# The opening of a fused Fourier-mixing and SiLU kernel: other buffers, another order and more filler products

## The chip, the core and the metric

The kernel runs on one core of one Trainium2 chip. The metric is the device time of one execution in microseconds (us). A core has TensorE (PE in the profile, its weight loads apart as PEld), VectorE (DVE), ScalarE (ACT), GpSimd (POOL), SyncE (SP, which here only issues transfers), and 16 DMA engines. An engine takes its instructions in the order in which the program gives them. ACT and POOL issue transfers too, and an issue that has to wait holds up what stands behind it on that engine.

## What is computed

```python
X = np.fft.rfft(x, axis=1)                      # x: 8 batches x 3008 x 256, float32
y = np.fft.irfft(X * (filt_r + 1j * filt_i)[None], n=3008, axis=1)
h = y.reshape(24064, 256) @ w_in                # w_in: 256 x 2048
out = (h / (1 + np.exp(-h))) @ w_out            # w_out: 2048 x 256
```

So each batch is filtered along its 3008 positions, and all 24064 rows then go through a two-layer network with SiLU between the layers.

## The kernel before, in words

**The body.** Each batch is cut into 6 pairs of token blocks (`PAIRS` for each half), and each pair is taken through 8 steps (`NJP`), one for each block of 256 hidden columns: 384 steps in all. A step is `hidden` (L639, seven products of 128x128 weights by 256 columns, a Strassen-like scheme with seven weight combinations for each 2x2 block) and `project` of the step before (L698, seven more). The combinations come from `combine_weights` (four additions or subtractions of 128x256; with `part` 0 or 1 it makes the first or the last two). While the steps of one batch run, the transform of the next is threaded between them: `put` and `plan` give each piece a step and an eighth of a step (a "round"), and `until` issues what is due.

**The transform of a batch** has four kinds of product: stage 1 (`pa`), `forward` (`pb`, L433), inverse (`pc`, L491) and `stage3` (`pd`, L538). Between `forward` and inverse, `multiply` (L448) takes the filter to the PSUM results, and between inverse and `stage3` the results go through DRAM (`d2`) to be regrouped.

**The opening** is what the change is about: batch 0 has no steps to hide behind. Its groups g = 0 to 5 go through these pieces, in an order written out by hand (L957 to L1013):

- `multiply(g, k)` for k = 0, 1 on DVE: a real and an imaginary filter product of 128x512 each, into a tile of the pool `z` (4 buffers) and one of the pool `p` (2 buffers; for k = 1 one of the pool `abc`).
- `inverse_first(g)` on PE: 16 products for each of 4 terms and 2 halves (groups 2 to 5), which read those tiles.
- `rows_first(g)`: for i = 0, 1 ACT copies a 128x512 result out of PSUM (L498) into a tile of the pool `q` (i = 0) or `o` (i = 1), 2 buffers each, and issues its store to `d2` (L501, 256 KB), on the ACT queue; for group 4 on the POOL queue.
- `load_t4(g, first, last)`: loads back, for g = 0 to 3, rows `first` to `last` of `d2` (L526). Rows 0 to 31 come from groups 0 to 3, rows 32 to 47 from groups 4 and 5. All issues are on the SP queue, but for one of the two halves of the last rows, which is on the ACT queue. The tiles for g = 2 and 3 stand where `neg[0]` and `neg[1]`, two tables of `inverse_first`, stood.
- `stage3(g)` for g = 0 to 3, and copies of its results to `y` (L549 on ACT, for g = 2 and 3 one on DVE L244 and one on ACT L246). With all eight copied, step 0 can begin.

**Weights.** The 16 blocks j of the weights come as raw float64 words. `load_weights(j)` (L816, L819) loads two halves of 256 KB each on SP; `split_weights` (DVE L835, L838; ACT L837, L839, and for some L844, L845), `round_weights` (DVE L851 to L857) and `place_weights` (L866) turn them into float32 in `w_t`. Blocks 0 and 1 are loaded into a tile of the pool `y`, blocks 2 and 3 into its other buffer. Their work is put between the pieces of the opening: `split(4, 5)` stands behind `inverse_first(5)` and ahead of `rows_first(3)`, and `combine_weights` of 0 and 1 are on POOL.

**x of batch 1.** `second["load_x"](u)` loads 384 KB into half `u` of `x_all` (L274, on SP). A `memset` of one element by POOL (L976) stands ahead of it. Stage 1 of batch 0 had its own last x in `x_all`, read for the last time by the L297 products that end at 29.42 us.

**Filler.** `idle(n)` (L918) makes n products of 96x128 by 128 whose result nobody reads. `idle(36)` stands at the start, `idle(20)` ahead of `stage3(0)`.

**PSUM.** In the opening `bank` hands out the eight banks in turn.

Of the kernel before, what the change touches and what calls it, by code (L numbers as in the profile page):

```python
# [46 lines left out]
FP32 = mybir.dt.float32  # L47
# [6 lines left out]
B, S, C = 8, 3008, 256  # L54
DFF = 2048
N1, N2 = 47, 64
NS, NG = 24, 6
# [110 lines left out]
def kernel(  # L168
# [31 lines left out]
    zpool = pool("z", 4)  # L200
# [22 lines left out]
    x_all = xpool.tile([128, 2, 2, 2 * C], FP32)  # L223
# [26 lines left out]
    def bank(b, name, spare=None):  # L250


        if b > 0 and spare is not None:
            return accps.tile([128, 2, C], FP32, name=name, tag=f"a{spare}")
        if b > 0 or early[0] is None:
            return fps.tile([128, 2, C], FP32, name=name, tag="f")
        early[0] += 1
        k = early[0] % 8
        if k < 2:
            return fps.tile([128, 2, C], FP32, name=name, tag="f")  # L260
        if k > 5:
            return xps.tile([128, 2, C], FP32, name=name, tag="x" if k == 6 else "yz")
        return accps.tile([128, 2, C], FP32, name=name, tag=f"a{k - 2}")

    def spectral(b):
# [4 lines left out]
        xs, us, t2s, banks, prods, halves, t4s = {}, {}, {}, {}, {}, {}, {}  # L270
# [168 lines left out]
            prods[g] = []  # L439

        def multiply(g, k):
            z = zpool.tile([128, 2, C], FP32, name=f"z_{b}_{g}_{k}", tag="z")
            if b == 0 and k == 1:
                pt = abcpool.tile([128, 3, C], FP32, name=f"p_{b}_{g}_{k}", tag="abc")[:, 0:2]
            else:
                pt = ppool.tile([128, 2, C], FP32, name=f"p_{b}_{g}_{k}", tag="p")
            for m, dst in ((0, z), (1, pt)):
                nc.vector.tensor_tensor(  # L448
                    out=dst, in0=banks[g][k],
                    in1=f_t[m][:, g, k:k + 1, :].to_broadcast([128, 2, C]), op=ALU.mult)  # L450
            prods[g].append((z, pt))
# [77 lines left out]
        def stage3(g):  # L529
# [17 lines left out]
            for h in range(2):  # L547
                if early[0] is not None and g < 2:
                    nc.scalar.copy(out=dst[:, :, h, n0:n0 + 4], in_=ps[h])  # L549
                else:  # L550
                    evac(dst[:, :, h, n0:n0 + 4], ps[h])

        return dict(load_first=load_first, stage1_first=stage1_first, load_x=load_x, sums=sums, stage1=stage1, reverse_x=reverse_x,
                    load_fold=load_fold, fold=fold, stage1_fold=stage1_fold, evict_fold=evict_fold,
                    load_t2=load_t2, forward=forward, multiply=multiply, add=add, inverse=inverse, inverse_first=inverse_first, rows_first=rows_first, even=even, rows=rows, load_t4=load_t4, stage3=stage3)

# [2 lines left out]
    def put(step, rnd, piece, *args):  # L559

        pending.append((step + rnd / ROUNDS, len(pending), lambda: piece(*args)))
# [234 lines left out]
    def load_weights(j):  # L796

        if j in (8, 13):
            raw = upool.tile([128, 2, 512], U32, name=f"raw_{j}", tag="u")
        else:  # L800

            if j in (0, 2):
                raws["at"] = ypool.tile([128, 2, HALF], FP32, name=f"raw_{j}", tag="y").rearrange(
                    "p a n -> p (a n)").bitcast(U32)[:, 0:2048]
                raws["y"] = raws["at"]
            elif j in (4, 11):
                raws["at"] = raws["s"] = spool.tile([128, 2048], U32, name=f"raw_{j}", tag="s")
            elif j == 6:
                raws["at"] = gpool.tile([128, 2048], U32, name=f"raw_{j}", tag="g")
            elif j in (9, 14):  # L810
                raws["at"] = raws["y"]
            elif j == 12:
                raws["at"] = raws["s"]
            at = 1024 * (j in (1, 3, 5, 7, 10, 12, 15))
            raw = raws["at"][:, at:at + 1024].rearrange("p (w n) -> p w n", w=2)
        nc.sync.dma_start(  # L816
            out=raw[:, 0].rearrange("p (a n) -> p a n", a=2),
            in_=moe_w_in.bitcast(U32)[:, 256 * j:256 * j + 256].rearrange("(a p) n -> p a n", p=128))
        nc.sync.dma_start(out=raw[:, 1], in_=moe_w_out.bitcast(U32)[128 * j:128 * j + 128, :])  # L819
        raws[j] = raw  # L820
# [55 lines left out]
    def combine_weights(jp, part=None, eng=None):  # L876

        eng = eng or v

        def w(c):  # L880
            return w_t[:, jp, c]
        if part != 1:
            combine(eng, w(S1), w(S3), w(A22), ALU.add)
            combine(eng, w(S2), w(S1), w(A11), ALU.subtract)
        if part != 0:
            combine(eng, w(S3), w(A11), w(S3), ALU.subtract)
            combine(eng, w(S4), w(A12), w(S2), ALU.subtract)
# [6 lines left out]
    def split(*js):  # L894
        if wide:
            split_weights(*js)
# [5 lines left out]
    def placed(*js, eng=None):  # L902
        if wide:
            place_weights(*js, eng=eng)
        else:
            for j in js:
                load_exact(j)
# [7 lines left out]
        for i in range(2):  # L915
            nc.gpsimd.memset(bias_t[32 * j:32 * j + 32, 3 + i:4 + i], 1.0 if j % 2 == i else -1.0)

    def idle(n):  # L918

        ps = bank(0, "idle").rearrange("p a c -> p (a c)")  # L920
        for _ in range(n):
            nc.tensor.matmul(out=ps[:, 0:128], lhsT=wx_t, rhs=wx_t, start=True, stop=True)

# [29 lines left out]
    for k in range(16):  # L953
        part["stage1_first"](k, 1)
        if k < 12:
            part["stage1_first"](k + 4, 0)
    placed(0, 1)  # L957
    for g in range(2):
        part["forward"](g)
    for g in range(NG):  # L960
        for k in range(2):
            part["multiply"](g, k)
        if g in by_gpsimd:
            for k in range(2):
                part["add"](g, k)
        if g + 2 < NG and g != 2:
            part["forward"](g + 2)
        if g == 0:
            part["inverse_first"](0)
            part["rows_first"](0)  # L970
        if g == 2:
            split(2, 3)
            rounded(2, 3)
            placed(2, 3, eng=gp)

            gp.memset(x_all[0:1, :, 0, 0:1], 0.0)  # L976
            for jp in (0, 1):
                combine_weights(jp, eng=gp)
            part["inverse_first"](1)
            part["forward"](4)  # L980
            part["inverse_first"](2)
            for done in (1, 2):
                part["rows_first"](done)
            for u in range(2):
                second["load_x"](u)
            weights(9, 10)
        if g == 4:
            part["inverse_first"](3)
    for g in (4, 5):
        part["inverse_first"](g)  # L990
    split(4, 5)
    for g in (3, 4, 5):
        part["rows_first"](g)
        if g == 3:
            for later in range(4):
                part["load_t4"](later, 0, 32)
    rounded(4, 5)
    placed(4, 5)
    split(6, 7)
# [7 lines left out]
    rounded(8)  # L1007
    placed(8)
    weights(11, 12, 13)
    idle(20)  # L1010
    for g in range(4):
        part["stage3"](g)
    early[0] = None  # L1013
# [7 lines left out]
    for j in range(9, NJ):  # L1021
        put(j - 9, 1, lambda j=j: (split(j), rounded(j)))
        put(j - 9, 5, placed, j)
        if j % 2:

            put(*((j - 8, 5) if j < 15 else (j - 9, 6)), combine_weights, j // 2, 0)
            put(*((j - 7, 5) if j < 13 else (j - 7 if j == 13 else j - 8, 1)), combine_weights, j // 2, 1)

        if j < 11:
            put(j - 9, 1, weights, j + 5)  # L1030
# [63 lines left out]
```

## Time and profile before

| what | value |
|---|---|
| median of 4 runs | 2598.08 us (2595.97 to 2600.65) |
| profiled execution, its own time | 2598.38 us |
| span of its trace | 2596.6 us |
| PE busy, share of the span | 2565.9 us, 99% |
| DVE, ACT, POOL busy | 1694.9, 1106.6, 425.9 us |
| granted PE clock, mean over the span | 0.995 |
| first product of `stage3`, first product of step 0 | 75.55 us, 84.59 us from the start of the span |

The profile lists, for groups of equal instructions, the busy time and what ended the idle time ahead of them. The timeline lists instructions by start and duration in us from the start of the span; an engine's name with a q stands for its queue (SPq, ACTq: an issue of a transfer), `xN` for N records. A float32 product has two records on PE. "PEclk" is the share of the full TensorE clock that was granted. Where a text below says that a transfer landed, the time is that of the last update of its semaphore in the trace.

### The profile page before, as it was taken

Reading aid. Unit: us, or ns where it says so; the run is one execution under the profiler, and the core shown is the slowest. Engines: PE = TensorE matmul, PEld = TensorE weight load, DVE = VectorE, ACT = ScalarE, POOL = GpSimd, SP = SyncE. Lnnn points to the kernel's source line nnn. Section 1 sums busy time; section 2 is a strip of 40 time slices with the busy share of each in tenths; the row PEclk is TensorE's granted clock in tenths of the full one; section 3 lists DMA queues with packets and bytes.
Section 4 is the critical chain, followed back from the end, with each engine's and each line's share of the span. In section 5 each row is a group of like instructions: output and inputs, shape, how many; then the busy total and the mean of one; then the engine's idle time right before and its main releaser. Section 6 shows DMA issues by size and latency. Waiting matters only on the chain.

```text
span 2596.6 us, 48346 instructions
## 1 busy us (share of the span) xinstructions
PE 2565.9 (99%) x18928; PEld 2188.3 (84%) x18928; DVE 1694.9 (65%) x3572; ACT 1106.6 (43%) x3015; POOL 425.9 (16%) x669
## 2 busy tenths in 40 slices
PE   8899999999999999999999999999999999999998
PEld 6688888888888888888888888888888888888987
DVE  7766666666666766667666676666766676555554
ACT  3544444444444444443444444444444444444443
POOL 2111211121112111211122111211122112100101
PEclk9899999999999999999999999999999999999999
DMA  8531232212222222232223222232223311211000
GB/s 273 143 90 44 67 80 66 66 52 80 65 57 66 74 65 58 57 82 66 63 57 80 66 66 57 72 76 57 62 70 72 70 46 29 58 21 21 9 17 16
DMA packets 200045, 171.08 MB, mean 66 GB/s; under 512 B 122084, under 2 KB 174164, under 8 KB 199028
## 3 DMA queue, kind: packets, MB, share of 16 engines
q1 hardware_dynamic: 178488, 117.04, 18.8%
q0 software_dynamic: 16928, 44.65, 5.5%
q10 hardware_dynamic: 4400, 6.29, 0.8%
q8 instruction: 149, 2.44, 0.4%
q14 instruction: 80, 0.66, 0.1%
HBM read 96.05 MB, written 81.26 MB: 68 GB/s over the span
## 4 chain that ended last, share of the span: by engine, by line
PE 95%; DMA 2%; DVE 1%; ACT 1%; issue 0%; SPq 0%; ACTq 0%; DVEq 0%
PE acc L711 43%; PE px L652 26%; PE pyz L652 19%; PE pd L538 3%; PE pb L433 2%; PE pc L469 2%; PE pf L403 1%; DVE g L623 0%; PE pa L340 0%; DMA w_t<-in_x_dram 0%; PE pc L491 0%; DMA t<-d 0%; DMA filt<-in_filt_i_dram 0%; DMA e_t<-e_tbl 0%; ACT t L344 0%
## 5 line engine op out<-in xcount | busy, mean ns | idle before, releaser
L711 PE MATMUL acc<-g,w_t 128*128 128x256 f32 (+1 forms) x5376 | 1512.1, 375 | 0.4 <-DVE g L623 0.4
L711 PEld LDWEIGHTS acc<-g,w_t 128*128 128x128 f32 x5376 | 1021.3, 190 | 115.7 <-DVE g L623 0.8
L623 DVE TENSOR_TENSOR g<-pyz,abc 128x256 f32<-128x256 f32 (+1 forms) x1152 | 480.2, 417 | 537.5 <-ACT abc L673 297.7
L623 DVE TENSOR_TENSOR g<-g 128x256 f32<-128x256 f32 (+3 forms) x1152 | 617.3, 536 | 196.8 <-ACT g L656 183.7
L652 PE MATMUL px<-ty,w_t 128*128 128x256 f32 (+1 forms) x2304 | 686.8, 380 | 0.8 <-ACT abc L673 0.5
L656 ACT ACTIVATE g<-g 128x256 f32<-128x256 f32 (+1 forms) x1152 | 473.0, 411 | 244.3 <-DVE g L623 244.3
L623 POOL TENSOR_TENSOR s<-s 128x256 f32<-128x256 f32 (+1 forms) x329 | 260.0, 808 | 1454.2 <-DVE s L731 1437.9
L652 PEld LDWEIGHTS px<-ty,w_t 128*128 128x128 f32 x2304 | 424.0, 190 | 83.5 <-issue 25.9
L652 PE MATMUL pyz<-y,w_t 128*128 128x256 f32 (+1 forms) x1536 | 453.7, 377 | 0.0
L652 PEld LDWEIGHTS pyz<-y,w_t 128*128 128x128 f32 x1536 | 283.4, 189 | 45.4 <-DVE g L623 4.8
L667 ACT COPY abc<-px 128x256 f32<-128x256 f32 (+1 forms) x384 | 141.5, 368 | 364.3 <-PE px L652 364.3
L656 ACT ACTIVATE g<-px 128x256 f32<-128x256 f32 (+1 forms) x384 | 146.1, 380 | 307.3 <-PE px L652 307.3
L673 ACT COPY abc<-px 128x256 f32<-128x256 f32 (+1 forms) x384 | 144.0, 375 | 309.7 <-PE px L652 309.7
L652 PE MATMUL px<-y,w_t 128*128 128x256 f32 (+1 forms) x768 | 229.8, 381 | 0.9 <-ACT y L246 0.9
L652 PE MATMUL pyz<-ty,w_t 128*128 128x256 f32 (+1 forms) x768 | 225.6, 375 | 0.0
L652 PEld LDWEIGHTS px<-y,w_t 128*128 128x128 f32 x768 | 142.1, 189 | 39.9 <-ACT g L656 15.4
L652 PEld LDWEIGHTS pyz<-ty,w_t 128*128 128x128 f32 x768 | 146.0, 190 | 16.9 <-DVE g L623 0.5
L660 ACT COPY abc<-px 128x256 f32<-128x256 f32 (+1 forms) x384 | 135.3, 352 | 2.7 <-PE px L652 1.3
L244 DVE COPY y<-pd 128x376 f32<-128x376 f32 x62 | 50.0, 807 | 103.7 <-PE pd L538 103.7
L538 PEld LDWEIGHTS pd<-wi_t,t 48*64 48x64 f32 x4096 | 68.8, 140 | 29.6 <-issue 29.6
L246 ACT COPY y<-pd 128x376 f32<-128x376 f32 x62 | 50.2, 810 | 88.6 <-PE pd L538 88.6
L538 PE MATMUL pd<-wi_t,t 48*64 48x47 f32 x4096 | 76.5, 239 | 10.0 <-DMA t<-d 9.4
(102 smaller groups left out, 1322.7 us busy)
## 6 DMA issues: line engine op xcount, KB each, us to landing
t<-d SPq DMA_DIRECT2D x120, 192.0 KB
d<-q POOLq DMA_DIRECT2D x86, 256.0 KB, 2.6
t<-d SPq DMA_DIRECT2D x84, 256.0 KB
out_dram<-o SPq DMA_DIRECT2D x636, 32.0 KB
d<-tf POOLq DMA_DIRECT2D x144, 96.0 KB, 2.4
xr<-in_x_dram SPq DMA_DIRECT2D x6, 1472.0 KB
x_all<-in_x_dram SPq DMA_DIRECT2D x72, 96.0 KB
x_all<-xr SPq DMA_DIRECT2D x72, 96.0 KB
```

The costliest lines, as they stand in the source:

```text
L244: nc.vector.tensor_copy(out=dst, in_=src)
L246: nc.scalar.copy(out=dst, in_=src)
L433: nc.tensor.matmul(out=ps[k][32 * j:32 * j + 32, ri, :], lhsT=d_t[rows, 4 * g + at, ri, :], rhs=t2[rows, at, :], start=True, stop=True)
L469: nc.tensor.matmul(out=ps[j][64 * k:64 * k + 64, a, :], lhsT=e_t[rows, g + a, k, ri, :], rhs=zs[k][rows, ri, :], start=(a == 0 and ri == 0 ...
L538: nc.tensor.matmul(out=ps[h][c0:c0 + 64, cb, i, :], lhsT=t4s[g][rows, i, 128 * cb + c0:128 * cb + c0 + 64], rhs=wi_t[rows, :], start=True, ...
L623: eng.tensor_tensor(out=out, in0=in0, in1=in1, op=op)
L652: nc.tensor.matmul(out=out, lhsT=w_t[:, jp, c, 0], rhs=rhs, start=start, stop=True, skip_group_check=True)
L656: nc.scalar.activation(out=g[:, k, 0:n], in_=g[:, k, 0:n] if src is None else src, func=AFT.Silu)
L660: nc.scalar.copy(out=sums[:, 0, 0:n], in_=xo)
L667: nc.scalar.copy(out=sums[:, 1, 0:n], in_=xo)
L673: nc.scalar.copy(out=sums[:, 2, 0:n], in_=xo)
L711: nc.tensor.matmul(out=acc[pair][i][:, h, 0:n], lhsT=w_t[:, jp, c, 1], rhs=g[:, k, 0:n], start=(jp == 0 and h == 0), stop=last, skip_group ...
```

## The change

It does the following.

1. The products of group 5 in batch 0 (`multiply(5, k)`) go to the 8 KB per partition into which the raw words of weight blocks 0 and 1 were loaded, and no longer to tiles of `z`, `p` and `abc`.
2. `idle` takes a tile to write to. `idle(8)` into group 1's first bank is put between the copies of `rows_first(1)` and `rows_first(2)`, and `idle(20)` becomes `idle(47)`.
3. x of batch 1 is loaded right behind the stage 1 products in the program, and the POOL `memset` goes.
4. `combine_weights(0)` moves from POOL to DVE, behind `split(4, 5)`.
5. `rows_first(3)` and the first loads of `load_t4` move ahead of `split(4, 5)`.
6. The last half of `combine_weights(6)` (for j = 13) moves from step 6, round 1 to step 5, round 7.

```diff
         def multiply(g, k):
-            z = zpool.tile([128, 2, C], FP32, name=f"z_{b}_{g}_{k}", tag="z")
-            if b == 0 and k == 1:
+            if b == 0 and g == NG - 1:
+
+                room = raws["first"].bitcast(FP32).rearrange("p (k i r c) -> p k i r c", k=2, i=2, r=2)
+                z, pt = room[:, k, 0], room[:, k, 1]
+            else:
+                z = zpool.tile([128, 2, C], FP32, name=f"z_{b}_{g}_{k}", tag="z")
+            if b == 0 and g == NG - 1:
+                pass
+            elif b == 0 and k == 1:
                 pt = abcpool.tile([128, 3, C], FP32, name=f"p_{b}_{g}_{k}", tag="abc")[:, 0:2]
...
                 raws["y"] = raws["at"]
+                raws.setdefault("first", raws["at"])
...
-    def idle(n):
+    def idle(n, ps=None):
-        ps = bank(0, "idle").rearrange("p a c -> p (a c)")
+        ps = (ps or bank(0, "idle")).rearrange("p a c -> p (a c)")
...
             part["stage1_first"](k + 4, 0)
+    for u in range(2):
+        second["load_x"](u)
     placed(0, 1)
...
             placed(2, 3, eng=gp)
-
-            gp.memset(x_all[0:1, :, 0, 0:1], 0.0)
-            for jp in (0, 1):
-                combine_weights(jp, eng=gp)
+            combine_weights(1, eng=gp)
             part["inverse_first"](1)
             part["forward"](4)
             part["inverse_first"](2)
-            for done in (1, 2):
-                part["rows_first"](done)
-            for u in range(2):
-                second["load_x"](u)
+            part["rows_first"](1)
+            idle(8, part["halves"][1][0])
+            part["rows_first"](2)
             weights(9, 10)
         if g == 4:
             part["inverse_first"](3)
     for g in (4, 5):
         part["inverse_first"](g)
+    part["rows_first"](3)
+    for later in range(4):
+        part["load_t4"](later, 0, 32)
     split(4, 5)
-    for g in (3, 4, 5):
+    combine_weights(0)
+    for g in (4, 5):
         part["rows_first"](g)
-        if g == 3:
-            for later in range(4):
-                part["load_t4"](later, 0, 32)
     rounded(4, 5)
...
-    idle(20)
+    idle(47)
     for g in range(4):
         part["stage3"](g)
...
-            put(*((j - 7, 5) if j < 13 else (j - 7 if j == 13 else j - 8, 1)), combine_weights, j // 2, 1)
+            put(*{13: (j - 8, 7), 15: (j - 8, 1)}.get(j, (j - 7, 5)), combine_weights, j // 2, 1)
```

More of the change, by code (lines that the diff above doesn't have):

```diff
@@ L551, in stage3 @@
                     evac(dst[:, :, h, n0:n0 + 4], ps[h])
-        return dict(load_first=load_first, stage1_first=stage1_first, load_x=load_x, sums=sums, stage1=stage1, reverse_x=reverse_x,
+        return dict(halves=halves, load_first=load_first, stage1_first=stage1_first, load_x=load_x, sums=sums, stage1=stage1, reverse_x=reverse_x,
                     load_fold=load_fold, fold=fold, stage1_fold=stage1_fold, evict_fold=evict_fold,
```

## The prediction

> **What bounds the kernel now.** I read the page first: PE is busy 99% of the span and 95% of the chain that ended last, so only what keeps PE waiting, or slow, is worth anything. A gain on DVE, ACT or POOL counts only through that.
>
> ```profile
> PE 2565.9 (99%) x18928; PEld 2188.3 (84%) x18928; DVE 1694.9 (65%) x3572; ACT 1106.6 (43%) x3015; POOL 425.9 (16%) x669
> PE 95%; DMA 2%; DVE 1%; ACT 1%; issue 0%; SPq 0%; ACTq 0%; DVEq 0%
> ```
>
> Then the table by stage, for the ramp (columns: stretch, length, busy time of PE, PEld, DVE, ACT and POOL with counts, granted clock, DMA share, GB/s):
>
> ```profile
> 50.00:60.00 10.00, 10.00 (x201) 6.88 (x193) 7.42 (x15) 3.67 (x7) 5.89 (x10) 1.00 0.93 290
> 60.00:70.00 10.00, 6.12 (x68) 5.29 (x60) 8.53 (x20) 7.54 (x13) 1.72 (x2) 0.92 0.66 218
> 70.00:80.00 10.00, 4.45 (x164) 4.48 (x165) 6.33 (x16) 3.33 (x6) 0.00 (x0) 0.50 0.93 224
> 80.00:90.00 10.00, 8.60 (x115) 6.22 (x110) 5.37 (x11) 4.94 (x10) 0.00 (x0) 0.55 0.10 34
> 90.00:100.00 10.00, 9.48 (x38) 6.65 (x37) 7.37 (x17) 5.74 (x15) 3.08 (x7) 1.00 0.42 133
> ```
>
> Between 60 and 90 us PE stands still and then works at half clock. Cut finer, the clock falls at 68.4 us and is back at 88.9. Last the timeline of PE, where a bracket is the idle time ahead and what ended it:
>
> ```profile
> 60.84 0.61 PE L491 MATMUL pc<-p,neg 64*64 64x256 f32 x8
> 61.39 4.73 PE L922 MATMUL idle<-wx_t 96*128 96x128 f32 x40
> 75.55 4.85 PE L538 MATMUL pd<-wi_t,t 48*64 48x47 f32 x166 [9.43 <-DMA t<-d]
> 80.93 2.79 PE L538 MATMUL pd<-wi_t,t 48*64 48x47 f32 x90 [0.53 <-issue]
> 84.59 1.22 PE L652 MATMUL px<-y,w_t 128*128 128x256 f32 x2 [0.88 <-ACT y L246]
> ```
>
> The inverse ends, twenty filler products run out, 9.43 us pass until `d2` is back, and stage 3 and step 0 run at half clock. From step 1 to the last steps I find one PE gap over 0.15 us, 0.27 us in step 6. So the change is worth what it does between 46 and 93 us, and whatever moves step 1 moves the end by as much.
>
> **The change, part by part.**
>
> *Buffers for group 5.* Its first filter product started at 53.74, after 1.65 us of waiting for group 3's inverse, and the next waited 0.20 more. The new tile was last read before 12 us. DVE gains 1.85 us; the four products cost 0.68 us each as before. PE gains nothing: the inverses run without a gap from 50.87 to 61.4 and read group 5 from 57.8. The gain buys the start of `split(4, 5)` on DVE at 54.6 instead of 56.43.
>
> *`combine_weights(0)` on DVE.* Four operations took 1.56 us on DVE (64.37, for block 2), and POOL took 5.82 us for eight. It eats 1.56 of the 1.85. It lies where DVE would wait for ACT's half of the split; without that cover it costs 1.56 us on DVE, whose ramp ends at 76.55 and is next wanted by stage 3's third group (81.89). POOL has nothing due between 56 and 63. Zero.
>
> *Order on ACT.* Today the copies of group 3 stand behind the split: ACT works on it from 56.88 to 60.62, and the copies start at 60.53, though the products were done at 54.6. Now they go first. They need the two buffers of group 1, whose stores landed at 53.04 and 53.85. But the moved x rows now go ahead of these stores: 2 x 384 KB, at 295 GB/s (2304 KB landed between 53.2 and 61.0) 2.6 us. So 55.6 and 56.5; the copies (0.59 us) and issues end at 57.4, 4.9 us earlier than today. The stores don't land as much earlier: transfers are busy 0.93 to 0.99 until 58, and what was issued by 54.27 landed until 60.99. Another 512 KB at that rate end at 62.7; today 64.12. The first loads of `t4` start 1.5 us earlier. The split (3.75 us) now follows, from 57.4 to 61.2, then the copies of groups 4 and 5; the last store is issued at about 64.1 (65.17) and lands 5.0 us later as today, at 69.1 (70.19).
>
> *x of batch 1.* It was issued at 50.31 and 50.70, and can now go at about 47.1, behind the raw words of block 8 (46.35). Nothing waits for it until step 0 (88.27). The same bytes go through, so its price is the place it takes from the stores. The trace shows that stores of ACT's queue wait behind older loads of SP's: one issued at 53.11 had its first packets down at 58.23 and landed at 59.62, between weight loads issued at 51.74 and 52.30. The Trainium skill, DMA: Bandwidth & Descriptors, section "Queues, rings and completion order", has each engine take turns between queues by packets; by that the moved rows would cost the stores half of the 2.6 us. This trace looks like order of issue. There is a second price. Transfers from SP and ACT use eight semaphores in turn, and an issue waits until the eighth before it has landed (ACT's 4.47 us at 53.54 is such a wait: the store at 53.11 waited for one that landed at 53.04). Two more issues ahead of group 1's stores put their waits on loads that landed at 49.59 and 50.45, up to 2.5 us after today's issues (47.13, 48.11). ACT then has 4.5 us of slack up to 53.1. I take zero for this; its upper bound is the slower rival below.
>
> *Second loads.* Today the last store lands at 70.19, and group 0's last rows at 75.28, 5.1 us later; SP was still held by a first load issued at 70.51. The fastest of these twelve loads took 3.2 us. With the first loads over earlier I take 4.3: stage 3 starts at 69.1 + 4.3 = 73.4. Bounds: 72 (below) and 75 (nothing of the landing gained, hold gone).
>
> *Filler.* A filler product takes 0.2235 us at full clock (two records 0.112 apart). 47 of them end at 61.4 + 10.5 = 71.9, so stage 3 can't start sooner, and today's 9.43 us without work become 1.5. The clock fell 2.3 us after the last product today. Gaps of 3.06 us (at 29.42) and of 1.63 and 0.61 us with one product between (at 47.02) left it at 1.00. So it most likely holds. The eight other products take 1.8 us from 47.0; group 5's `forward` has its first product at 48.65 and its second bank at 49.84, so 0.2 us is lost and then covered. Zero.
>
> *At full clock.* Stage 3 needs 64 records a group, four each 0.107 us at half clock and four each 0.0583 later (164.4): 1.71 and 0.93 us. Four groups end 4.0 us after the start. ACT has two copies for each of the first two groups and one for each of the others; from 1.1 us they take 0.73 each and end at 5.6, against 9.04 us today from stage 3 to step 0: 3.4 us gained. Step 0 to step 1 took 8.0 us (84.59 to 92.59), and the clock came back at 88.9. At full clock the third product waits for DVE's two token results (1.35 us), four stage 1 products take 1.7, and from the fifth product on it is 2.3 as today: 6.2, so 1.8 us gained.
>
> A rule that speaks against this: the Trainium skill, TensorE: Matmul & The Clock Gate, "What's actually happening", frees the clock after about 3.4 us of sustained work. By it, today's stage 3 would have had full clock from 79 us, and step 0 would have nothing to gain. The rows say otherwise: 4.85 us of stage 3 without a gap stayed at 0.50.
>
> *Step 6.* The gap at 137.5 follows two DVE operations (0.75 us) of the moved half, ahead of block 15's split. Moved, it goes: 0.27 us. If other DVE work is late instead: zero.
>
> *Sum* against the profiled execution's 2598.38 us: 2.15 (stage 3 from 75.55 to 73.4) + 3.4 + 1.8 + 0.27 = 7.6, so **2590.8 us**. That execution lies 0.3 us above the median of the runs, which I leave in. With stage 3 at 72 and at 75 it is 2589.4 and 2592.4.
>
> **Rivals.**
>
> *The clock falls all the same* (0.27). For it: after the filler and the stage 3 products PE stands still again for some 1.5 us each, and if `d2` is back at 74.5, the first gap is 2.6 us, longer than today's 2.3 from last product to fall. Against it: 3.06 us at 29.42. Then stage 3 starts 1.05 us earlier, step 6 gives 0.27, and perhaps 1 us of the half-clock time goes: 2596. With `d2` no earlier than today, 2598.
>
> *x in the way* (0.07), the slower side. If the stores of group 2 get the semaphores of the moved x rows, and these land at 57.2 as today, ACT's second copy of group 2 moves from 53.54 to 57.3; PE needs that bank for group 4's inverse, which started at 54.37. All after it moves by up to 3.7 us, less what is won above: stage 3 at 78, filler done at 75.6, the clock falls in the gap, and the end comes 2.5 - 0.27 us later: 2600.6. It decides once stage 3 starts after 75.55; over 0.2% needs 80.5.
>
> *The filler itself is the bound* (0.06). If the loads land by 71, stage 3 starts at 71.9: 2589.3.
>
> **How the numbers follow.** The forecast (2589.4 to 2592.4) has 0.60, the others what stands beside them. The range 2588.5 to 2597.5 takes in the forecast, the filler case and most of the first rival. A measurement of this kernel tells 0.2% (5.2 us) from no change, so faster is under 2592.9: forecast and filler case, but for the forecast's late end, 0.60. Slower is the far end of its rival and what I haven't seen, 0.04; the rest, 0.36, is within.
>
> **What would show it.** Filler of L922 ending near 71.9 and stage 3 (L538) at 73 to 74; PEclk 1.00 in every stretch from 60 to 100; stage 3 to step 0 in 5.6 us, step 0 to 1 in 6.2; group 3's copies (L498) at 55 to 57, group 4's inverse still at 54.4; no gap in step 6. I am wrong if the clock column shows 0.50 after 72, if the copies of group 2 or 3 wait for x rows, or if stage 3 starts after 75.5.

## The result, and the profile after

| | kernel before | kernel after |
|---|---|---|
| median of all runs | 2598.41 us (52 runs, 2595.15 to 2605.8) | 2595.92 us (34 runs, 2593.29 to 2599.75) |
| profiled execution, its own time | 2598.38 us | 2596.58 us |
| span of its trace | 2596.6 us | 2594.8 us |
| stage 3 starts | 75.55 us | 74.91 us |
| stage 3 to step 0 | 9.04 us | 8.42 us |
| step 0 to step 1 | 8.00 us | 7.56 us |

The ratio is 0.999 with a 95% interval of 0.9985 to 0.9994: the change makes the kernel faster by a tenth of a per cent, 2.5 us in the medians where I had forecast 7.6. In the two profiled executions it is 1.8 us. PE is still what bounds the kernel. First the page of the kernel after, busy times and shares of the chain that ended last:

```profile
PE 2572.2 (99%) x18998; PEld 2193.2 (85%) x18998; DVE 1696.4 (65%) x3576; ACT 1106.6 (43%) x3015; POOL 422.7 (16%) x664
PE 95%; DMA 2%; DVE 1%; ACT 1%; issue 0%; ACTq 0%; SPq 0%; POOL 0%; DVEq 0%; POOLq 0%
```

PE has 70 more records, which are filler (8 and 27 products of two records each), so its 6.3 us of added busy time are no work. The table by stage of the kernel after, in the columns that the prediction gave:

```profile
50.00:60.00 10.00, 9.60 (x181) 6.36 (x184) 8.48 (x18) 2.38 (x5) 4.32 (x7) 1.00 1.00 305
60.00:70.00 10.00, 10.00 (x118) 8.99 (x111) 8.21 (x19) 9.11 (x16) 1.33 (x2) 1.00 0.69 231
70.00:80.00 10.00, 8.43 (x252) 8.17 (x252) 8.16 (x20) 4.81 (x8) 0.00 (x0) 0.83 0.72 191
80.00:90.00 10.00, 7.12 (x65) 4.38 (x55) 6.05 (x13) 4.85 (x10) 0.42 (x1) 0.83 0.13 44
90.00:100.00 10.00, 9.89 (x42) 7.51 (x41) 7.65 (x20) 5.66 (x15) 3.59 (x8) 1.00 0.58 176
```

The clock column is what the filler was expected to mend, and for the most part it did: 0.83 and 0.83 between 70 and 90 us, where the kernel before had 0.50 and 0.55. But look at the PE column: 7.12 us of 10 between 80 and 90, less than the 8.60 of before. PE got its clock and then stood still. The timeline of PE for the kernel after says where:

```profile
62.60 10.76 PE L930 MATMUL idle<-wx_t 96*128 96x128 f32 x94
74.91 5.33 PE L545 MATMUL pd<-wi_t,t 48*64 48x47 f32 x222 [1.54 <-DMA t<-d]
81.66 0.72 PE L545 MATMUL pd<-wi_t,t 48*64 48x47 f32 x34 [1.42 <-issue]
83.33 1.19 PE L659 MATMUL px<-y,w_t 128*128 128x256 f32 x2 [0.95 <-ACT y L246]
```

The 9.43 us without work are 1.54. The stop in the middle of stage 3, put down to "issue" (PE waited for nothing that the profile shows), was 0.53 us in the kernel before and is 1.42 us now, and it has moved from behind the 166th record of stage 3 to behind the 222nd. Cut finer, the clock is at half twice from 70 us on, from 76.35 to 79.76 and from 83.18 to 86.59 (and once earlier, from 31.98 to 35.39, which the profile of before does not have). From the start of step 1 on, the two traces run alike: 2495.8 us to the end of the last product in both, and in every kernel below. So all that the change does lies ahead of step 1, as I had said.

So two things were to be explained: the stop, and the falls of the clock. My theory for the stop: PE takes its instructions in blocks of 256 records (of PE and PEld together), and stage 3 uses them up faster than the next block comes. The rival: late transfers (weights loaded beside stage 3) or late copies. The page has one row that bears on it, the queue by which instructions come, with packets, MB and share of the DMA engines' time:

```profile
q8 instruction: 149, 2.44, 0.4%
```

2.44 MB in 149 packets are 16 KB each, and 2 x 18998 records of PE and PEld, cut into blocks of 256, are 148.4 blocks.

### The profile page after: what moved, and what is told of

The parts are those of the page before. It is cut to its first block, busy times and chain, and to the rows that moved or that the text cites. A ratio compares the mean times of both kernels' runs of the same rounds, so it can differ in the third digit from the quotient of the medians.

```text
span 2594.8 us, 48483 instructions
## 1 busy us (share of the span) xinstructions
PE 2572.2 (99%) x18998; PEld 2193.2 (85%) x18998; DVE 1696.4 (65%) x3576; ACT 1106.6 (43%) x3015; POOL 422.7 (16%) x664
## 3 DMA queue, kind: packets, MB, share of 16 engines
q8 instruction: 149, 2.44, 0.4%
## 4 chain that ended last, share of the span: by engine, by line
PE 95%; DMA 2%; DVE 1%; ACT 1%; issue 0%; ACTq 0%; SPq 0%; POOL 0%; DVEq 0%; POOLq 0%
PE acc L718 43%; PE px L659 26%; PE pyz L659 19%; PE pd L545 3%; PE pb L433 2%; PE pc L476 2%; PE pf L403 1%; DMA x_all<-in_x_dram 1%; PE pa L340 0%; DMA w_t<-in_x_dram 0%; DVE g L630 0%; DMA filt<-in_filt_r_dram 0%; PE pc L498 0%; DMA d<-q 0%; DMA filt<-in_filt_i_dram 0%
```

## The experiments

The kernels were timed in three groups of four, each beside runs of the kernel before on the same chip; those runs had a median of 2598.53 us in the first group, 2596.79 in the second and 2597.08 in the third. The kernel after was in none of the three, so it can be set beside the kernels below only by way of these medians. How far such ratios can be trusted is seen in the last experiment, where the kernel before is held against itself.

### Filler alone

The kernel before, with one edit.

```diff
-    idle(20)
+    idle(47)
```

> The kernel before with 47 filler products for 20, nothing else. Filler theory (what was missing was work for PE): the filler ends at 72, stage 3 still starts at 75.5, and the clock holds at least in some executions: 2595 to 2596. Fetch theory (PE stops in stage 3 when it crosses into its next 16 KiB of instructions, and every stop opens a gap in which the clock can fall): 3.5 us without work stay ahead of stage 3, a stop of 0.5 to 1.5 us stays in it, and the clock is at 0.50 in stage 3 or step 0 or both: 2597 to 2598.5.

Measured: 2601.12 us, ratio 1.0011 (1.0003 to 1.002). The timeline of PE:

```profile
64.08 10.76 PE L922 MATMUL idle<-wx_t 96*128 96x128 f32 x94
78.73 6.86 PE L538 MATMUL pd<-wi_t,t 48*64 48x47 f32 x239 [3.89 <-DMA t<-d]
86.41 0.77 PE L538 MATMUL pd<-wi_t,t 48*64 48x47 f32 x17 [0.82 <-issue]
```

What follows: without earlier data the filler leaves a gap of 3.89 us, the clock falls at 78.07 and is back at 91.73. Filler alone buys nothing. Part of this profile's late start is older than the filler (the first `forward` product stood at 34.40 us, 1.9 us later than in the kernel before). Why the kernel should be slower, and not just no faster, I have not settled; see the run with 30 products.

### The order alone

The kernel after, with the filler of before.

```diff
-            idle(8, part["halves"][1][0])
...
-    idle(47)
+    idle(20)
```

> The changed kernel with 20 filler products for 47 and without the eight; its buffers, order and early x stay. Filler theory: all of the gain goes, 2597.5 to 2598.5. Order theory (the gain is that stage 3 starts sooner): stage 3 still starts about 1 us sooner than in the kernel before, and 1 to 1.5 us of the 2.5 stay: 2597.

Measured: 2596.24 us, ratio 0.9993 (0.9985 to 1.0002). PE:

```profile
64.18 4.73 PE L930 MATMUL idle<-wx_t 96*128 96x128 f32 x40
73.11 7.50 PE L545 MATMUL pd<-wi_t,t 48*64 48x47 f32 x256 [4.20 <-DMA t<-d]
81.48 1.22 PE L659 MATMUL px<-y,w_t 128*128 128x256 f32 x2 [0.88 <-ACT y L246]
```

What follows: the change without its filler (buffers, orders, early x, step 6) stands 2.3 us under the kernel before in the medians, about what the whole change brings, though the interval takes in 1. A gain from the filler is not shown. Read the second row against the kernel after. Here the clock is at half from 72.16 to 85.81, so all of stage 3 is slow, and it has no stop at all. From stage 3's first record to its last it takes 7.18 us; in the kernel after, half of it at full clock, 7.24. What the kernel after won by a faster clock it gave back as a stop.

### The weights behind stage 3

The kernel after; the last raw weights, whose loads ran beside stage 3, are issued behind it.

```diff
-    weights(11, 12, 13)
     idle(47)
     for g in range(4):
         part["stage3"](g)
+    weights(11, 12, 13)
```

> The changed kernel with the loads of weight blocks 11 to 13 (1.5 MB) behind stage 3 in the program. Fetch theory: PE's next 16 KiB of instructions no longer lie behind these loads (in the changed kernel their packet started at 79.3, about 2.9 us after PE had crossed into its last block, and PE stood from 80.24 to 81.66): the stop shrinks to 0.5 us or less, 2594.5 to 2595. If the stop is something else: no change, 2595.9. If the blocks come too late for steps 2 to 4: slower, with waits of the split for its words.

Measured: 2596.09 us, ratio 0.9995 (0.9986 to 1.0004). PE:

```profile
73.47 1.35 PE L545 MATMUL pd<-wi_t,t 48*64 48x47 f32 x66 [0.62 <-DMA t<-d]
75.18 2.53 PE L545 MATMUL pd<-wi_t,t 48*64 48x47 f32 x156 [0.36 <-DMA t<-d]
80.34 0.72 PE L545 MATMUL pd<-wi_t,t 48*64 48x47 f32 x34 [2.63 <-issue]
82.01 0.97 PE L659 MATMUL px<-y,w_t 128*128 128x256 f32 x2 [0.95 <-ACT y L246]
```

What follows: this is the execution that I had forecast. Stage 3 starts at 73.47 (73.4 in the prediction), and the clock is 1.00 from 37.87 until 82.25. And yet stage 3 needs 8.54 us to step 0, not 5.6. Without the weight loads in its way the stop is longer, 2.63 us, and it stands behind the same record: 66 + 156 = 222. So the loads of the weights are not what makes it.

In this trace PE entered the block that ends there at 75.58 us, used it up by 77.48, its next packet ran from 78.11 to 79.08, and PE went on at 80.34. The stop is what is left of a delay. From the entry into a block until PE goes on with the next one passed 4.30 us (kernel before), 4.92 (after), 4.76 (here), and 4.2 to 5.1 in the five other kernels that stop. In all of them PE went on 1.3 to 1.6 us after the end of the packet, and that is the ground for saying that it waits for this packet. (In the kernel after the packet started 2.5 us after the entry, not 2.9 as the expectation has it.) Using the 256 records took some 3.4 us at half clock and 1.9 at full. The difference is the stop. What sets the length of the delay, no run shows.

### Whole columns in stage 3

The kernel after, with the 4 x 64 products of 48x64 weights of each group made as 4 x 16 of 48x128, half as many records for the same results. `n` is the width.

```diff
-                    for c0 in (0, 64):
+                    n = 128 if b == 0 and g < 4 else 64
+                    for c0 in range(0, 128, n):
...
-                                out=ps[h][c0:c0 + 64, cb, i, :],
-                                lhsT=t4s[g][rows, i, 128 * cb + c0:128 * cb + c0 + 64],
+                                out=ps[h][c0:c0 + n, cb, i, :],
+                                lhsT=t4s[g][rows, i, 128 * cb + c0:128 * cb + c0 + n],
```

> The changed kernel with stage 3 of the opening in products of 48x128 in place of two of 48x64: half of the instructions, 256 records in place of 512. Fetch theory: at most one block is crossed in stage 3, the stop goes or shrinks, stage 3 to step 0 takes 6 us and not 8.4: 2593 to 2594. If PE's own rate is the bound and there is no stop for instructions: the same time or slower, as two products at a time take the place of four: 2595.9 or more.

Measured: 2600.05 us, ratio 1.0007 (0.9998 to 1.0016). PE:

```profile
64.44 10.76 PE L931 MATMUL idle<-wx_t 96*128 96x128 f32 x94
75.25 12.07 PE L546 MATMUL pd<-wi_t,t 48*128 48x47 f32 x128
88.19 1.22 PE L660 MATMUL px<-y,w_t 128*128 128x256 f32 x2 [0.88 <-ACT y L246]
```

What follows: with 256 records in stage 3 (PE and PEld) instead of 512 the stop is gone. That fits the blocks but doesn't decide, as it was gone at half clock in the order alone too. And the records of the wide products come only every 0.0558 us at full clock, where four of the narrow ones came every 0.0583: 1.79 us a group against 0.93. And the clock fell at 77.94, though PE was busy in 99% of the 3.41 us before, and stayed at half until 91.60. All groups wide is too much.

### Half of the groups with whole columns

The same, for groups 2 and 3 alone.

```diff
-                    n = 128 if b == 0 and g < 4 else 64
+                    n = 128 if b == 0 and g in (2, 3) else 64
```

> The changed kernel with products of 48x128 in stage 3's groups 2 and 3 alone. At full clock a group of 48x64 products takes 0.93 us for 256 records of PE and PEld, one of 48x128 products took 1.79 us for 128. Fetch theory, in its form after late_weights (a block of 256 records is asked for when PE enters the one before it, and is there 4.3 to 5.2 us later whatever else the transfers do): 384 or so records fit into the two blocks that are there, no stop in stage 3, and it lasts 5.4 to 5.6 us at full clock, not 7.4: 2594 to 2595. Where the clock falls in the gap ahead of stage 3 the gain is lost, since 48x128 products take twice as long as 48x64 ones: 2597. If the stop isn't a matter of the number of instructions it stays, and the time is 2597 or more.

Measured: 2593.53 us, ratio 0.999 (0.9981 to 1.0). PE:

```profile
62.29 10.76 PE L931 MATMUL idle<-wx_t 96*128 96x128 f32 x94
72.98 5.79 PE L546 MATMUL pd<-wi_t,t 48*64 48x47 f32 x192
79.74 0.67 PE L660 MATMUL px<-y,w_t 128*128 128x256 f32 x2 [0.96 <-ACT y L246]
```

What follows: with 384 records PE reaches step 0 before the block ends; stage 3 runs without a stop, and takes 6.76 us to step 0, at full clock. (A group has 128 records of PE and PEld with narrow products and 64 with wide ones; the expectation gives twice that, but its total of 384 is right.) This is 1.7 us shorter than in the kernel after, part of whose stage 3 ran at half clock, and 0.6 to 1.8 us shorter than in the four kernels that had full clock nearly to the end of their narrow stage 3 (7.40 us with early filler, 7.51 with late x, 8.32 with the split first, 8.54 with late weights), although half of the products go at half the rate. Of all kernels here its profiled execution has the shortest span, 2591.5 us. So the stop is a matter of how many records PE uses up in a time. In this execution taking records away paid even at a price in PE time; the interval for the kernel's time just reaches 1.

### x of batch 1 late

The kernel after, with x at its place of before, and the `memset` with it.

```diff
-    for u in range(2):
-        second["load_x"](u)
     placed(0, 1)
...
+            gp.memset(x_all[0:1, :, 0, 0:1], 0.0)
             combine_weights(1, eng=gp)
...
             part["rows_first"](2)
+            for u in range(2):
+                second["load_x"](u)
             weights(9, 10)
```

> The changed kernel with the x rows of batch 1 loaded where the kernel before loads them, behind the stores of group 2 and held by the POOL memset; all else as changed. If the early x rows hold up ACT's stores (in the changed kernel two stores of group 2 were issued at 55.84 and 57.52, within 0.1 us of the landing of the two x loads): the copies of group 3 come 2 us or more sooner, stage 3 starts up to 1 us sooner and the time is 2595 or less. If the transfers are what takes the time, in whatever order: 2595.9, as changed.

Measured: 2594.68 us, ratio 0.9993 (0.9983 to 1.0002). PE:

```profile
72.19 3.98 PE L545 MATMUL pd<-wi_t,t 48*64 48x47 f32 x222
77.99 0.82 PE L545 MATMUL pd<-wi_t,t 48*64 48x47 f32 x34 [1.81 <-issue]
79.71 1.20 PE L659 MATMUL px<-y,w_t 128*128 128x256 f32 x2 [0.90 <-ACT y L246]
```

What follows: moving x early is worth nothing that the times can tell, in either direction (2.1 us under the kernel before without it, 2.5 with it). My slower rival's mechanism is there, however. ACT in the kernel after, where group 1's second store has just been issued:

```profile
52.11 0.59 ACT L505 COPY q<-pc 128x512 f32<-128x512 f32 x1 [2.96 <-DMA raw<-in_moe_w_out_dram]
55.84 0.33 ACTq L508 DMA_DIRECT2D d<-q  x1
56.26 0.59 ACT L505 COPY q<-pc 128x512 f32<-128x512 f32 x1 [3.56 <-DMA raw<-in_moe_w_out_dram]
57.52 0.33 ACTq L508 DMA_DIRECT2D d<-q  x1
57.95 0.59 ACT L505 COPY q<-pc 128x512 f32<-128x512 f32 x1 [1.10 <-DMA x_all<-in_x_dram]
```

Group 2's copy ended at 52.7, and its store was issued at 55.84, when the first x rows had landed (55.76); the second store at 57.52, behind the other rows (57.45). The profile names a weight load for the wait ahead of 56.26; the landing time says x. It cost ACT 3 us of the slack that I had counted, and PE's inverse nothing: group 5's, which needs these banks, began at 59.04. But it moved what stands behind it on ACT. Group 3's copies began at 57.95 and the last store was issued at 66.18; in the kernel with late x these are 54.56 and 63.91, and stage 3 starts at 72.19 instead of 74.91.

### Filler behind stage 1

The kernel after, with 12 filler products in a gap of some 3.2 us ahead of the first `forward` product, where the clock fell at 31.98 in the kernel after, and in the first four kernels above at 33.57 to 34.61.

```diff
+    idle(12)
     for u in range(2):
         second["load_x"](u)
```

> The changed kernel with 12 more filler products (2.7 us) behind the stage 1 products, in the gap of 3.1 to 3.3 us in which five of six profiles show the clock fall for one window of 3.41 us. If that fall reaches the end: the inverse ends 28.9 us after the first forward product in place of 29 to 31, and the time is 2595. If stage 3 waits for the transfers and not for PE: no change, 2595.9.

Measured: 2595.69 us, ratio 0.9995 (0.9986 to 1.0005). The half-clock stretch moved to 38.89 and was as long, 3.41 us; no gain. The stop (2.05 us) stood behind the 199th record of stage 3 instead of the 222nd. Twelve products are 24 records on PE and 24 on PEld, so the boundary should come 24 records of PE earlier, behind the 198th; it does, within a record. That is the plainest sign of what the stop is: filler that ran 40 us earlier moves it by as many records as it has.

### The split first

The kernel after, with its `split(4, 5)` and `combine_weights(0)` back ahead of group 3's copies, and the other parts kept.

```diff
+    split(4, 5)
+    combine_weights(0)
     part["rows_first"](3)
     for later in range(4):
         part["load_t4"](later, 0, 32)
-    split(4, 5)
-    combine_weights(0)
```

> The changed kernel with the split of blocks 4 and 5 and combine_weights(0) ahead of the copies of group 3 again. Order theory (the copies of group 3 ahead of the split are what makes stage 3 start sooner): group 3's stores are issued 3 to 4 us later, the first loads of t4 start 2 us later, stage 3 starts 1.5 us later and the time is 2597.5. If the order on ACT is worth nothing because the stores land only when the older transfers are through: 2595.9.

Measured: 2596.09 us, ratio 0.9998 (0.9988 to 1.0007): 0.7 us under the kernel before, where the kernel after had 2.5. Stage 3 started at 73.24, with a stop of 2.36 us behind the 222nd record. The interval is too wide to price the order on ACT by itself. The medians put most of the gain on it, but the profile doesn't: stage 3 started neither 1.5 us later, as the order theory has it, nor later at all than in the kernel after (74.91). What the order on ACT is worth stays open.

### Mixed columns and a bridge to step 0

Groups 2 and 3 wide, and four filler products in the 0.96 us between stage 3 and step 0.

```diff
         part["stage3"](g)
+    idle(4)
     early[0] = None
```

> The changed kernel with 48x128 products in groups 2 and 3 of stage 3, and four filler products behind the last of them. Theory (the clock goes down by stretches of 3.41 us with too little work, and 0.96 us without work between stage 3 and step 0 are enough for it): with the gap filled the clock stays at 1.00 from stage 3 to step 1, step 0 to step 1 takes 6.2 to 6.8 us instead of 7.64, and the time is about 1 us under that of the same kernel without the four products, 2592 to 2593. Rival (the fall there has to do with something else, or the four products come in the way of step 0): a half-clock stretch again behind 79 us, or step 0 later by up to 0.9 us, and a time of 2593.5 to 2594.5.

Measured: 2593.94 us, ratio 0.9985 (0.9976 to 0.9994), the best ratio of this study. The profiled execution can't tell the two theories apart: it was the longest of the eleven (2602.78 us; the next 2595.95). Its last store landed at 74.24, and PE shows what that does:

```profile
62.62 10.76 PE L931 MATMUL idle<-wx_t 96*128 96x128 f32 x94
77.08 10.95 PE L546 MATMUL pd<-wi_t,t 48*64 48x47 f32 x192 [3.70 <-DMA t<-d]
87.96 2.08 PE L931 MATMUL idle<-wx_t 96*128 96x128 f32 x8
```

A gap of 3.70 us, half clock from 75.30 to 92.37, and 10.95 us of stage 3 where the execution above took 5.79. Whether the bridge does what it was put in for stays open; the medians of the two mixed kernels, each 3.1 to 3.3 us under the kernel before of its group, give no sign of it. That they beat the kernel before by more than the kernel after does is what the medians say, and the intervals overlap.

### Mixed columns and a shorter filler

Groups 2 and 3 wide, without the bridge, and five filler products fewer ahead of stage 3.

```diff
-    idle(47)
+    idle(42)
```

> The changed kernel with 48x128 products in groups 2 and 3 of stage 3, and 42 filler products ahead of it instead of 47. Theory (stage 3 starts at the later of two ends, that of the filler and that of the loads): the filler ends 1.1 us earlier, stage 3 starts where group 0's rows have landed, 0.5 to 1.1 us earlier, and the time is 2592.5 to 2593. By the reading of PE's stops as instruction blocks of 256 records, the 20 records that the filler lacks put the boundary in stage 3 twenty records later, and still without a stop. Rival (the loads are the bound, and the gap lets the clock fall): half clock in stage 3, and 2594 to 2596.

Measured: 2597.45 us, ratio 0.9998 (0.999 to 1.0007). My theory fell, and the rival had it. PE:

```profile
62.55 9.64 PE L931 MATMUL idle<-wx_t 96*128 96x128 f32 x84
75.00 10.38 PE L546 MATMUL pd<-wi_t,t 48*64 48x47 f32 x192 [2.81 <-DMA t<-d]
86.35 1.19 PE L660 MATMUL px<-y,w_t 128*128 128x256 f32 x2 [0.96 <-ACT y L246]
```

The loads were the bound, the gap was 2.81 us, and the clock fell at 76.08 for 13.65 us. The eleven executions fall into groups by their granted clock: three with 0.997 took 2593.4 us in the mean, seven with 0.996 took 2598.4, and one with 0.995 took 2601.2. With five filler products fewer the first kind was rare; with 47, nine of eleven executions had 0.997 or more in the bridge kernel, and seven of ten in the mixed kernel without the bridge.

### Thirty filler products

The kernel before, with `idle(30)` for `idle(20)`.

> The kernel before with 30 filler products instead of 20, nothing else. With 47, it was 1.0011 times as long as before. Theory (the filler costs nothing as long as it ends before the loads land; what that profile showed at 34.4 us was chance): stage 3 at 75.5, half clock in it as before, and a time within 0.7 us of the kernel before. Rival (each filler product costs something, by its instructions or by shifting the stops): about 10/27 of 2.6 us, 1 us longer than before.

Measured: 2599.03 us, ratio 1.0006 (0.9997 to 1.0015): between the two, and not told from 1. In its profile the data are again what stage 3 waits for (6.81 us), and the stop is where it should be:

```profile
78.49 4.26 PE L538 MATMUL pd<-wi_t,t 48*64 48x47 f32 x146 [6.81 <-DMA t<-d]
83.76 3.23 PE L538 MATMUL pd<-wi_t,t 48*64 48x47 f32 x110 [1.02 <-issue]
```

Behind 146 records instead of 166: ten products are 20 records earlier. With 47 the boundaries come behind 112 and 240, and that profile had its stop behind 239. The kernel before itself, run once more in this group (next experiment), took as long: 2599.13 us. So no cost of the ten products can be read here. Whether 27 of them in the old order cost a microsecond or two, and why, stays open.

### The kernel before once more

> The kernel before, unchanged, for a second profile. In nine profiles of kernels that differ from it only behind 45 us the clock fell at 32 to 39 us, behind the last stage 1 product, and in the one profile of the kernel before it did not. Theory (the stretches of 3.41 us begin elsewhere in each execution): a half-clock stretch of 3.41 us at 32 to 35 us in this one too, most likely, and the stop in stage 3 again behind 1730 records of PE, as long as its packet is late. Rival (the change brought that fall on): full clock to 68 us again. The time is that of the kernel before, 1.000.

Measured: 2599.13 us, ratio 1.0003 (0.9994 to 1.0012). Two medians of one kernel in one group differ by 2 us; less than that, in a single group, is nothing. PE:

```profile
63.14 4.73 PE L922 MATMUL idle<-wx_t 96*128 96x128 f32 x40
76.96 6.40 PE L538 MATMUL pd<-wi_t,t 48*64 48x47 f32 x256 [9.09 <-DMA t<-d]
84.26 0.67 PE L652 MATMUL px<-y,w_t 128*128 128x256 f32 x2 [0.90 <-ACT y L246]
```

The same instructions, and another execution: the clock fell at 33.51, which the first profile lacked; it was back in the middle of stage 3, at 81.29, where the first had to wait until 88.91; and the block boundary behind record 166 cost 0.14 us, because its packet had landed at 80.48 and PE came to it at 81.4. Stage 3 to step 1 took 13.85 us here and 17.05 there. Step 1 begins at 90.81 us here and at 90.89 in the profile of the kernel after, and the spans are 2594.7 and 2594.8: beside this profile of before, that of after shows no gain at all. The gain rests on the 86 timed executions, and the profiles show only where time goes. One profile is one draw. (Of the nine profiles in the expectation one, that with late x, had no fall behind stage 1 either.)

## Why the prediction was right or wrong

**Where the change acts: right.** Everything ahead of step 1, nothing behind it but the gap in step 6. That gap of 0.27 us is gone, but a new one of 0.19 us stands at 133.18, and from step 1 to the end the two traces differ by 0.05 us: the 0.27 didn't come.

**Buffers and `combine_weights(0)`: right but for the size.** DVE in the kernel after:

```profile
53.22 2.48 DVE L455 TENSOR_TENSOR raw<-pb,filt 128x512 f32<-128x512 f32 x4
55.61 0.42 DVE L843 TENSOR_SCALAR scratch<-raw 128x512 uint32<-128x512 uint32 x1
...
56.96 1.55 DVE L630 TENSOR_TENSOR w_t<-w_t 128x256 f32<-128x256 f32 x4
61.25 0.69 DVE L859 SCALAR_TENSOR_TENSOR scratch<-raw,scratch 128x512 f32<-128x512 uint32 x1 [2.74 <-ACT scratch L847]
```

Group 5's four products run without a wait, the four operations take 1.55 us, and DVE still waits 2.74 us for ACT behind them. The split starts at 55.61, 0.8 us earlier than in the kernel before and not 1.8.

**Start of stage 3: right in size, late in the profile.** I had the last store issued at 64.1, landed at 69.1, stage 3 at 73.4. In the profile of after these are 66.18, 72.35 and 74.91, in that of the mixed kernel 63.99, 69.09 and 72.98. Ten kernels have the changed opening, whole or in part: in six stage 3 starts between 72.19 and 73.50, in the four others, the kernel after among them, between 74.91 and 77.08. The term that I put at nothing is what was late in the profile of after: ACT's issues had to wait for the x rows, which landed at 55.76 and 57.45, so that group 3's first copy stands at 57.95 and not at 55.6, and the last store comes 2.1 us late. In the four late profiles the last store was issued at 66.18 to 67.77, in the six others at 63.91 to 65.89. The second loads took 2.7 us (72.35 to 75.08), not 4.3. The third rival, the filler as bound, is what happened in late x, mixed and early filler, where no wait stands ahead of stage 3. Of 2.15 us the profiled pair shows 0.64.

The filler of after ended at 73.36 and not at 71.9, since the inverse ended 1.2 us later than in the profile of before. The half-clock stretch at 31.98 fits that: the two profiles without such a stretch behind stage 1 (before, late x) end their inverse at 61.5 and 61.4, the twelve with one at 61.9 to 64.8.

**Stage 3 to step 0 in 5.6 us: wrong, and the main fault.** "Four groups end 4.0 us after the start" took the rate of 64 records in 0.93 us from a later place and let it go on for four groups. The rate was right: in the early filler's profile the four groups start at 73.50, 74.46, 75.39 and 76.33. But stage 3 has 512 records on PE and PEld, two blocks, and at that rate PE uses up a block in 1.9 us, while the next one came 4.2 to 5.1 us after the one ahead was entered. So full clock wins only a part of what I had counted. Measured to step 0: 8.42 us in the profile of after, 7.40 (early filler) to 8.54 (late weights) in its relatives with full clock, 8.38 at half clock without a stop (order alone). 0.62 us of the 3.4 came. The 0.53 us before "issue" stood in the profile of before, in a line that I quoted, and I didn't ask what it was.

The Trainium skill, Runtime: NRT & Kernel Launch, "Instruction fetch mechanics", says that a block of 256 instructions is fetched while the one ahead is executed, and that crossing a boundary is mostly hidden. The traces agree with the first: the packet follows the entry into the block ahead by 0.8 to 2.5 us. With the second they agree only where using up 256 records takes about as long as the next block: in stage 3 crossing cost nothing in the order alone, and 0.14 to 2.63 us in nine other profiles.

**Step 0 to step 1 in 6.2 us: wrong.** 7.56 us, because the clock fell at 83.18, behind the stop of 1.42 us and the 0.95 us for the last copies. Even without a stop (mixed) it fell at 80.31, and step 0 to 1 took 7.64. 0.44 us of the 1.8 came.

**The clock "most likely holds": wrong in its reason.** I judged by the length of a gap: 3.06 us had left the clock at 1.00. All stretches at half clock in these fourteen profiles, but for the last of each, which the end of the record cuts, are 3.41 us long or a multiple of it (6.83, 10.24, 13.65, 17.07, 20.48), and so are those at full clock (the first lasted 23.89 us, seven times 3.41, in eleven of the fourteen). So the clock is decided once in 3.41 us, at instants that lie elsewhere in each execution. What counts is the work in such a stretch; how much of it is needed, these runs don't show. (No share of busy time parts all cases: 53% of `forward` products kept the clock, 99%, most of it wide products of stage 3, did not.) In the kernel after, PE was busy in 54% of the 3.41 us ahead of 76.35, and the clock fell, with a gap of only 1.54 us. In the first profile of before, counted back from 68.43, two stretches meet at 30.88 and share the 3.06 us, so that PE was busy in 57% and 53% of them; in its second profile one stretch ahead of 33.51 held nearly the whole gap, 3% of work, and the clock fell.

With this, the row that I held against the skill's rule (TensorE: Matmul & The Clock Gate, "What's actually happening") doesn't speak against it. The page has a free-running window of 3413 ns, and the stretches agree. Counted from the fall at 68.43, the 4.85 us of stage 3 lie in a window with 0.29 us missing at its start and one with the stop in it; the first full one was 85.50 to 88.91, and the clock came back at its end. But a busy window isn't always enough: 3.41 us filled with 128 records of stage 3 released the clock in the kernel after (79.76) and in the second profile of before (81.29), and 124 and 128 such records did not in the order alone (78.98) and the filler alone (84.90). The wide products never did.

**Rivals, range and luck.** The forecast proper, 2589.4 to 2592.4, was missed by 3.5 us. That 2595.92 lies inside the wider range is luck: the range took in most of the first rival, "the clock falls all the same", which is nearest with 2596 us by its working, but has no stop in it and reached the number by other terms. "x in the way" has the wait right and the consequence wrong. Banks are handed out in turn, so group 2's go next to group 5's inverse and not to group 4's; PE waited for none of it, and the delay went by ACT's later stores instead. Of my three signs of being wrong two came: half clock after 72 us, and copies of group 2 that waited for x rows.

## What to carry to other kernels

Count the records in a stretch, not only their time: where PE would go through 256 records of PE and PEld in less than the 3.7 to 5.1 us that the next block took here, part of what a faster clock gains goes into waiting for instructions, and fewer, larger products can be worth more than a higher rate. A short wait that the profile puts down to "issue" is to be followed up, by its place in the count of records. Filler holds the clock if it fills the stretch until the data land, in the late executions too; with five products fewer it was lost in most executions.

## What was not expected of the hardware

- An engine's instruction stream as a bound: 4.2 to 5.1 us from entering a block of 256 records to going on with the next, in eight kernels with a stop, and the stop always within a record of a multiple of 256 from the others (behind some 1729 or 1985 records of PE, PEld and PE's queue from the start).
- The scatter between executions of one kernel goes with its granted clock: 97 executions of the kernel before ran in the three groups; the 22 with 0.994 took 2600.0 us in the mean, the 14 with 0.997 took 2595.6. That is more than the change is worth. In the kernel after the order is less clear (2595.7 us at 0.996, 2596.2 at 0.997, 2594.7 at 0.998); that the stop takes the clock's place there is a guess. In the mixed one with the shorter filler it is 5.0 us between 0.996 and 0.997.
- At full clock one record of a 48x128 product came every 0.0558 us, where four records of 48x64 products came every 0.0583, so the wide ones make the same results at half the rate.
